# A linear-attention and gated-FFN kernel: another order of loading, casting and filling at the start, and a new order of the whole program

## The chip, the core and the metric

The kernel runs on one core of one Trainium2 chip. TensorE (PE) multiplies matrices into PSUM; its weight loads are listed as PEld. VectorE (DVE) and ScalarE (ACT) work element by element, GpSimd (POOL) hardly computes here and issues loads that also convert the type, and SyncE (SP) issues loads and stores. Each engine takes its instructions strictly in its own order and waits on semaphores for the others. The metric is the device time of one execution in microseconds (us).

## The reference

For 8 batches, 8 heads, 576 positions and a head size of 64, in float32:

```
kv  = einsum('bhsd,bhse->bhde', k, v)
out = einsum('bhsd,bhde->bhse', q, kv)
x   = out / sqrt(mean(out*out over e) + 1e-6) * g_norm        # heads side by side: 512 columns
h   = relu(x @ w_in)                                          # w_in 512 x 1024
c   = conv_w[0]*h[s-1] + conv_w[1]*h[s] + conv_w[2]*h[s+1]    # along positions, zero outside
y   = (h * sigmoid(c)) @ w_out                                # w_out 1024 x 512, float32 out
```

## The kernel before, in words

The program is written out as a list of some 850 short words, `ORDER` (lines 59 to 135). Each word calls a small function, for example `hk.0.1.0.0@4`: function `hk`, arguments batch 0, column block 1, half 0, part 0, and a place (a PSUM bank or a slot of a ring of buffers) behind the `@`. The last lines of the kernel tie each instruction to the one before it on its engine, so the order of the words is the order on every engine: no scheduler changes it.

One batch goes through these steps. `Lq`, `Lk`, `Lv` load q, k and v through POOL's queue, converting to bf16. `kv` multiplies k and v (64 x 64 products, L402), and `kva` (ACT, L416) or `kvd` (DVE, L414) copies the result to bf16. `qt` transposes q on PE (L433), `qd` or `qa` copies it. `ot` forms the output of attention (L460), `sq` squares it on ACT (L509), `on` or `oq` sums the squares with a matrix of ones on PE: `on` with two products on the whole array (L528), `oq` with four on quarters of it (L537). `nl` takes the reciprocal root on ACT (L545), `mo` multiplies on DVE and writes x (L556). A batch is cut into halves u (heads) and s (positions), so x has four quarters. `hk`, `hs` or `hm` multiply x by w_in (L658, L628, L613), and `rp`, `rh` or `re` apply relu on ACT. The convolution is `ta`, `aa`, `ab` on DVE (L681 to L692), for four blocks of batch 0 it is `cv` on PE (L708). `sg` (or `sc` after `cv`) is the sigmoid on ACT (L698, L715), `mg` the gate on DVE (L722), `om` the product by w_out, in two parts of four blocks (L732). `ea` or `ed` copies a row block out of PSUM on ACT or DVE (L738, L743), `st` stores it through SP's queue. `oh`, `eh`, `dh`, `sh` do the same in halves for the last row block. Batches 4 to 7 sum the squares of two batches at once (`ss`, `ln`, `sl`, `sp`, `mu`), and batches 6 and 7 transpose q by DMA (`tq`).

Batch 0 is special. Its q, k and v come in float32 through SP's and ACT's queues in the order of `HEAD` (line 233), in pieces: q in four (heads u, positions s; `q.1.0` is u = 1, s = 0), k in four, v in two. `cad` (DVE) and `caa` (ACT) convert them (L384, L386). POOL's loads, w_in first, start behind `gt.k.1.0`, a copy that waits for the piece k.1 (L378). Products of zeros that nobody reads, `fi` (L286), stand on PE between the steps of the start. `ct` transposes the convolution's weights, `pg` and `pc` prepare them, `dg` builds diagonal matrices for `cv`; `ps`, `pl` and `pn` build constants that are read much later, by batches 4 to 7.

Of the kernel before, what the change touches and what calls it, by code (L numbers as in the profile page):

```python
# [58 lines left out]
ORDER = """  # L59
pre@0,1 af cad.q.0.0@0 cad.v.0.0@0 fi.10.512@0 qt.0.0.0@2 qd.0.0.0@0 gt.k.1.0 Li.0.4 fi.9.512@0 ct@0 Lq.1.0.2@1  # L60
Lk.1.0.2@0 Lv.1.0.2@1 Li.4.4 ps pg fi.4.512@1 cad.k.1.0@1 caa.v.1.0 caa.k.0.0 kv.0.0.1@4 kva.0.0.1@0 ot.0.0.0@6 pc
cad.v.3.0 cad.k.2.0 fi.2.512@0 cad.k.3.0 caa.q.1.0 qt.0.1.0@2 qd.0.1.0@1 sq.0.0.0@0 oq.0.0.0@4 fi.2.512@0 dg.1
caa.v.2.0 kv.0.1.1@0 fi.2.512@2 nl.0.0.0@0 kva.0.1.1 ot.0.1.0@4 sq.0.1.0@1 cad.q.0.1 qt.0.0.1@2 qa.0.0.1 fi.2.512@0
oq.0.1.0@0 nl.0.1.0@1 mo.0.0.0@0 cad.q.1.1 qt.0.1.1@6 qd.0.1.1 mo.0.1.0 ot.0.0.1@2 sq.0.0.1@2 ot.0.1.1@6 fi.1.512@0
sq.0.1.1@3 oq.0.0.1@0 nl.0.0.1@2 fi.1.512@4 fi.1.512@4 hk.0.1.0.0@4 hk.0.1.0.1 rp.1.0@0 on.0.1.1@0 nl.0.1.1@3
hk.0.2.0.0@5 hk.0.2.0.1 rp.2.0 dg.3 mo.0.0.1 dg.2 hk.0.3.0.0@4 hk.0.3.0.1 hk.0.0.0.0@2 hk.0.0.0.1 rp.0.0 hk.0.0.1.0@3
rp.3.0 hk.0.1.1.0@5 hk.0.3.1.0@0 mo.0.1.1 hk.0.3.1.1 rp.3.1 hk.0.1.1.1 rp.1.1 hk.0.0.1.1 rp.0.1 dg.0 hk.0.2.1.0@1
hk.0.2.1.1 qt.1.0.0@6 kv.1.0.1@4 rp.2.1 cv.0.2@2 sc.0.2@0 cv.0.3@0 qd.1.0.0@2 kvd.1.0.1@1 ot.1.0.1@6 sc.0.3 pl
sq.1.0.1@4 cv.0.1@4 cv.0.0@2 Lq.1.2.2 Lk.1.2.2 Lv.1.2.2 sc.0.1@1 fi.2.512@0 qt.1.1.0@0 qd.1.1.0@3 mg.0.1.1 Lo.0.8
sc.0.0 mg.0.1.0 oq.1.0.1@4 nl.1.0.1@4 mo.1.0.1@1 fi.1.512@2 hk.0.5.1.0@2 hk.0.5.0.0@3 hk.0.5.0.1 rp.5.0 hk.0.5.1.1  # L70
rp.5.1 ta.0.1.5@0 hk.0.4.1.0@0 hk.0.4.1.1 rp.4.1 hk.0.7.0.0@1 hk.0.7.0.1 kv.1.1.1@4 kvd.1.1.1 rp.7.0 ot.1.0.0@2
sq.1.0.0@5 hk.0.7.1.0@6 hk.0.7.1.1 rp.7.1 ta.0.1.7@1 ot.1.1.1@0 sq.1.1.1@6 oq.1.0.0@4 nl.1.0.0@5 mo.1.0.0 hk.0.4.0.0@6
hk.0.4.0.1 rp.4.0 hk.0.6.1.0@7 hk.0.6.1.1 rp.6.1 oq.1.1.1@4 nl.1.1.1@6 mo.1.1.1 hk.0.6.0.0@6 Lq.2.0.4@2 hk.0.6.0.1
rp.6.0 ta.0.1.4 hk.1.6.1.0@7 ta.0.1.6 hk.1.0.1.0@2 ot.1.1.0@4 sq.1.1.0@7 aa.0.1.2 hk.1.1.1.0@3 hk.1.2.1.0@6 hk.1.6.1.1
rh.1.6.1 hk.1.1.1.1 rh.1.1.1 on.1.1.0@0 nl.1.1.0@7 mo.1.1.0 hk.1.2.1.1 hk.1.5.1.0@7 hk.1.5.1.1 rh.1.5.1 rh.1.2.1
hk.1.3.1.0@3 hk.1.3.1.1 rh.1.3.1 hk.1.0.1.1 rh.1.0.1 ab.0.1.2 sg.0.1.5 sg.0.1.4 qt.2.1.0@0 qt.2.0.0@6 hk.1.5.0.0@3
hk.1.5.0.1 rh.1.5.0 qd.2.0.0@4 hk.1.0.0.0@2 hk.1.4.1.0@4 hk.1.4.1.1 hk.1.0.0.1 hk.1.1.0.0@5 hk.1.6.0.0@6 hk.1.1.0.1
hk.1.2.0.0@7 hk.1.2.0.1 rh.1.2.0 rh.1.1.0 rh.1.0.0 hk.1.6.0.1 rh.1.6.0 aa.0.1.3 qd.2.1.0@0 ab.0.1.3 sg.0.1.7 sg.0.1.6
hk.1.7.0.0@0 mg.0.1.2 hk.1.7.1.0@1 hk.1.7.1.1 rh.1.7.1 hk.1.7.0.1 rh.1.7.0 ta.1.1.1@0 ta.1.1.0 Lk.2.0.4@1 Lv.2.0.4@0
Lq.3.0.4@0 Lk.3.0.4@0 Lv.3.0.4@1 Lq.4.0.4@1 aa.1.1.0 hk.1.4.0.0@3 om.0.1.0.4@2 rh.1.4.1 hk.1.4.0.1 rh.1.4.0  # L80
om.0.2.0.4@5 kv.2.0.2@6 mg.0.1.3 om.0.1.4.4 ab.1.1.0 sg.1.1.0 sg.1.1.1 kvd.2.0.2@2 ot.2.0.1@0 sq.2.0.1@0 ed.0.1@0
# [57 lines left out]
def kernel(  # L139
# [142 lines left out]
    @op  # L282
    def fi(n, w):
        ps = bank()
        for _ in range(n):
            nc.tensor.matmul(ps[:, :w], zero[:, :P], zero[:, :w], start=True, stop=True)  # L286
# [538 lines left out]
```

## Time and profile before

| | us |
|---|---|
| median of 3 runs (lowest to highest) | 177.75 (177.67 to 177.93) |
| span of the profiled execution, first to last instruction | 175.6 |
| difference, outside the span | 2.2 |
| PE, DVE, ACT busy | 167.9, 149.5, 148.9 |
| POOL busy | 22.2 |

The profile gives of the profiled execution its span, 175.6 us; what a timed run has beyond it lies ahead of the first and behind the last instruction, so changes are reckoned against the span and carried over to the median. A line of the timeline reads: start, duration, engine, line, operation, what it writes and reads, how many in a row, and in square brackets how long the engine stood idle and for whom. A line of the chain has start, duration, engine and line. A line of the stages has the stretch, its length, and for each engine the busy time and the number of instructions, then granted clock, busy share of the DMA engines and their GB/s.

### The profile page before, as it was taken

The numbers are of one execution on the slowest core, as the hardware profiler recorded it, in microseconds if no ns is written. First come the engines' busy times: TensorE is split into PE (matmuls) and PEld (weight loads), VectorE is DVE, ScalarE is ACT, GpSimd is POOL, SyncE is SP. The second block draws the span as 40 slices with busy tenths as digits, with TensorE's granted clock in tenths as the row PEclk, the third lists the DMA queues.
The fourth block names the chain that finished last, engine by engine and source line by source line (L and its number), as shares of the span: only waits on it lengthen the run. The fifth ranks groups of instructions, "written<-read, shape, count | busy, mean of one in ns | idle before, by whom it ended". The sixth has DMA issues, their size and how long they took to land.

```text
span 175.6 us, 5070 instructions
## 1 busy us (share of the span) xinstructions
PE 167.9 (96%) x2097; PEld 100.0 (57%) x2114; DVE 149.5 (85%) x290; ACT 148.9 (85%) x268; POOL 22.2 (13%) x35
## 2 busy tenths in 40 slices
PE   7979999999999999999999999999999999999992
PEld 2334766676447677644467764444877744444451
DVE  2796638899688899999999998989999999999950
ACT  2368899999978999999999998999999967676721
POOL 3094512200603013030000000000000000000000
PEclk9999999999999999999999999999999999999999
DMA  5999999999999999999999050330310003064486
GB/s 159 392 323 207 207 207 207 208 208 209 207 241 230 227 207 207 170 182 197 258 181 161 14 134 0 119 123 0 119 63 0 0 0 116 13 239 175 179 304 237
DMA packets 25911, 29.11 MB, mean 166 GB/s; under 512 B 6036, under 2 KB 20384, under 8 KB 25888
## 3 DMA queue, kind: packets, MB, share of 16 engines
q0 software_dynamic: 13296, 14.50, 49.2%
q1 hardware_dynamic: 12048, 13.11, 26.2%
q10 hardware_dynamic: 544, 1.18, 1.7%
q8 instruction: 16, 0.26, 0.6%
q14 instruction: 7, 0.06, 0.1%
HBM read 32.52 MB, written 9.44 MB: 239 GB/s over the span
## 4 chain that ended last, share of the span: by engine, by line
PE 76%; DVE 12%; ACT 5%; DMA 3%; issue 3%; ACTq 0%; DVEq 0%
PE banks L732 32%; PE banks L628 14%; PE banks L613 9%; PE banks L658 4%; DMA stg<-in_v_dram 3%; PE banks L460 3%; DVE h L722 2%; PE banks L708 2%; ACT taps L698 2%; PE banks L402 2%; PE banks L593 2%; PE banks L433 1%; PE banks L528 1%; DVE taps L681 1%; PE banks L286 1%
## 5 line engine op out<-in xcount | busy, mean ns | idle before, releaser
L732 PE MATMUL banks<-w_out_sb,h 128*128 128x512 bf16 x267 | 62.8, 379 | 1.2 <-issue 0.6
L698 ACT ACTIVATE taps<-taps,cw 128x576 bf16<-128x576 bf16 (+1 forms) x44 | 40.6, 958 | 5.7 <-DVE taps L692 5.5
L732 PEld LDWEIGHTS <-h 128*128 128x128 bf16 x280 | 26.2, 98 | 30.0 <-issue 1.1
L628 PE MATMUL banks<-x,w_in_sb 128*128 128x288 bf16 (+2 forms) x256 | 34.2, 286 | 0.0
L640 ACT ACTIVATE h<-banks 128x288 bf16<-128x288 f32 (+2 forms) x80 | 29.5, 460 | 0.3 <-PE banks L658 0.2
L628 PEld LDWEIGHTS <-w_in_sb 128*128 128x128 bf16 x256 | 24.4, 98 | 7.8 <-issue 0.8
L722 DVE TENSOR_TENSOR h<-h,taps 128x1152 bf16<-128x1152 bf16 (+1 forms) x24 | 22.8, 952 | 1.2 <-ACT taps L698 1.2
L687 DVE TENSOR_TENSOR taps<-taps 128x1152 bf16<-128x1152 bf16 (+1 forms) x22 | 21.5, 978 | 0.5
L509 ACT ACTIVATE sq<-banks 128x576 bf16<-128x576 f32 (+2 forms) x32 | 20.8, 691 | 1.1 <-PE banks L460 1.1
L692 DVE TENSOR_TENSOR taps<-taps,h 128x1152 bf16<-128x1152 bf16 (+1 forms) x22 | 21.4, 972 | 0.3
L681 DVE TENSOR_SCALAR taps<-h,cw 128x576 bf16<-128x576 bf16 (+1 forms) x44 | 18.7, 424 | 0.6 <-ACT h L665 0.5
L682 DVE TENSOR_SCALAR taps<-h,cw 128x576 bf16<-128x576 bf16 (+1 forms) x44 | 18.4, 418 | 0.0
L738 ACT ACTIVATE row<-banks 128x512 f32<-128x512 f32 x23 | 13.5, 597 | 5.7 <-PE banks L732 4.2
L658 PE MATMUL banks<-x,w_in_sb 128*128 128x288 bf16 (+2 forms) x128 | 17.7, 286 | 0.1
L613 PE MATMUL banks<-x,w_in_sb 128*128 128x288 bf16 x128 | 16.9, 286 | 0.0
L556 DVE SCALAR_TENSOR_TENSOR x<-banks,cw,rs 128x576 bf16<-128x576 f32 (+2 forms) x16 | 13.0, 816 | 3.9 <-ACT rs L545 3.6
L658 PEld LDWEIGHTS <-w_in_sb 128*128 128x128 bf16 x128 | 12.0, 98 | 4.4 <-issue 0.5
L227 ACT ACT_TABLE_LOAD x10 | 12.8, 1283 | 2.0 <-issue 1.8
L613 PEld LDWEIGHTS <-w_in_sb 128*128 128x128 bf16 x128 | 12.3, 98 | 3.7 <-issue 0.2
L443 DVE COPY qT<-banks 128x1152 bf16<-128x1152 bf16 (+2 forms) x13 | 8.8, 681 | 5.7 <-PE banks L433 5.7
L545 ACT ACTIVATE rs<-banks,eps_sb 128x576 f32<-128x576 f32 (+2 forms) x16 | 11.8, 740 | 1.1 <-PE banks L528 1.1
L599 DVE SCALAR_TENSOR_TENSOR x<-o,cw,banks 128x576 bf16<-128x576 f32 (+2 forms) x16 | 12.1, 810 | 0.7 <-PE banks L593 0.5
(89 smaller groups left out, 162.9 us busy)
## 6 DMA issues: line engine op xcount, KB each, us to landing
out_dram<-row SPq DMA_DIRECT2D x35, 256.0 KB, 2.3
q_sb<-in_q_dram POOLq DMA_DIRECT2D x6, 576.0 KB, 17.9
k_sb<-in_k_dram POOLq DMA_DIRECT2D x6, 576.0 KB, 14.5
v_sb<-in_v_dram POOLq DMA_DIRECT2D x6, 576.0 KB, 17.9
stg<-in_v_dram ACTq DMA_DIRECT2D x2, 576.0 KB, 6.2
stg<-in_k_dram SPq DMA_DIRECT2D x4, 288.0 KB, 6.9
w_in_sb<-in_moe_w_in_dram POOLq DMA_DIRECT2D x2, 512.0 KB, 9.9
w_out_sb<-in_moe_w_out_dram POOLq DMA_DIRECT2D x1, 1024.0 KB, 15.5
```

Of the source, the lines that this page charges most:

```text
L509: nc.scalar.activation(T["sq", b, u, s], T["o", b, u, s], AX.Square)
L613: nc.tensor.matmul(ps[:, s, :HS], w_in_sb[:, t, f * P:(f + 1) * P], T["x", b][:, t, c0:c1], start=(t == 0), stop=(t == NT - 1))
L628: nc.tensor.matmul(ps, w_in_sb[:, t, f * P:(f + 1) * P], T["x", b][:, t, c0:c1], start=(t == 0), stop=(t == NT - 1))
L640: nc.scalar.activation(h, fr, AX.Relu)
L658: nc.tensor.matmul(T[at], w_in_sb[:, t, f * P:(f + 1) * P], T["x", b][:, t, c0:c1], start=(t == 0), stop=(t == NT - 1))
L681: nc.vector.tensor_scalar_mul(tap[:, 0, f % 2, :n, 8:8 + S], h[:, f], cw[:, f:f + 1])
L682: nc.vector.tensor_scalar_mul(tap[:, 1, f % 2, :n, :S], h[:, f], cw[:, 2 * NF + f:2 * NF + f + 1])
L687: nc.vector.tensor_add(tap[:, 1, :, :n, :S], tap[:, 0, :, :n, 7:7 + S], tap[:, 1, :, :n, 1:1 + S])
L692: nc.vector.tensor_add(y, y, span(b, n)[:, 2 * j:2 * j + 2])
L698: nc.scalar.activation(y, y, AX.Sigmoid, scale=cw[:, NF + f:NF + f + 1])
L722: nc.vector.tensor_mul(h, h, tap_of(b, j)[:, 1, :, :n, :S])
L732: nc.tensor.matmul(T["om", p, m], h[:, f, m * P:(m + 1) * P], w_out_sb[:, f, :], start=(f == 0), stop=(f == NF - 1))
```

## The change

The words of `ORDER` are put in another order from the first to the last, and some are exchanged for others. The parts that can be named:

- SP's queue at the start loads k.2 and k.3 ahead of q.1.0 (`HEAD`).
- The first half of w_in is loaded by two instructions of two column blocks each (`Li.0.2`, `Li.2.2`) where there was one of four. Behind it POOL loads v, k, q of batch 1 (it was q, k, v), and later the whole of batch 2's q, v, k ahead of w_out (it was w_out first).
- Seven converting copies of the start are on ACT and five on DVE (it was four and eight); `qa.0.0.0` copies the first transposed q on ACT. `pl`, `pn` and `ps` stand at DVE's start.
- A new word, `ff`, is like `fi` with float32 operands. The products of zeros are now `ff.4.256`, `ff.3.256`, `ff.1.128`, `ff.2.256`, `ff.1.128`, `ff.1.192`, `ff.1.256` and, on bf16, seven `fi` words, all ahead of the first `hk`. Before, `fi` words of 34 products of 512 columns stood ahead of it and three behind.
- Six `on` words became `oq`; `kva` and not `kvd` copies for batches 2, 3 and 6; `ea` took the place of `ed` for five row blocks, `ed` of `ea` for four.
- `oq` and `on` take one bank where the result fits in one (`pair`). The functions `ad` and `y_of` are new, but no word calls `ad`, so they change nothing that runs.

```diff
 ORDER = """
-pre@0,1 af cad.q.0.0@0 cad.v.0.0@0 fi.10.512@0 qt.0.0.0@2 qd.0.0.0@0 gt.k.1.0 Li.0.4 fi.9.512@0 ct@0 Lq.1.0.2@1
...
+pre@0,1 af pl pn ps caa.q.0.0@0 caa.v.0.0@0 ff.4.256@0 qt.0.0.0@0 qa.0.0.0@0 caa.k.0.0@0 cad.v.1.0 ff.3.256@2
+ff.1.128@2 ct@0 pg pc caa.k.1.0 gt.k.1.0 Li.0.2 caa.v.2.0 ff.2.256@1 ff.1.128@1 kv.0.0.1@2 Li.2.2 dg.1 kva.0.0.1@0
...
+    def pair(n):
+        if 2 * n <= 512:
+            return bank()[:, :2 * n].rearrange("p (e n) -> p e n", e=2)
+        return bank2()[:, :, :n]
...
-    HEAD = (("sync", "q.0.0 k.0.1 k.1.1 q.1.0 k.2.1 k.3.1 q.0.1 q.1.1"), ("scalar", "v.0.2 v.2.2"))
+    HEAD = (("sync", "q.0.0 k.0.1 k.1.1 k.2.1 k.3.1 q.1.0 q.0.1 q.1.1"), ("scalar", "v.0.2 v.2.2"))
...
     @op
+    def ff(n, w):
+        ps, z = bank(), zero.bitcast(FP32)
+        for _ in range(n):
+            nc.tensor.matmul(ps[:, :w], z[:, :P], z[:, :w], start=True, stop=True)
...
     def on(b, u, s):
         c0, c1 = cols(b, s)
-        ps = T["on", b, u, s] = bank2()[:, :, :c1 - c0]
+        ps = T["on", b, u, s] = pair(c1 - c0)
...
     def oq(b, u, s):
         c0, c1 = cols(b, s)
-        ps = T["on", b, u, s] = bank2()[:, :, :c1 - c0]
+        ps = T["on", b, u, s] = pair(c1 - c0)
```

Where the instructions stand now is shown at three places.

ACT at the start, before: the loads of v, the table of functions, then the copies of batch 0 (`v_sb`, `k_sb` and `q_sb` are the bf16 copies of the float32 pieces `stg` and `stq`, `kvb` the copied product of k and v, `sq` the squares, `rs` the reciprocal root).

```order
L227 ACT_TABLE_LOAD
L386 ACTIVATE v_sb<-stg 128x576
L386 ACTIVATE k_sb<-stg 128x576
L416 ACTIVATE kvb<-banks 128x2x64
L386 ACTIVATE q_sb<-stq 128x2x256
L509 ACTIVATE sq<-banks 128x2x256
L386 ACTIVATE v_sb<-stg 128x576
L545 ACTIVATE rs<-banks,eps_sb 128x2x256
```

The same place now:

```order
L232 ACT_TABLE_LOAD
L398 ACTIVATE q_sb<-stq 128x2x256
L398 ACTIVATE v_sb<-stg 128x576
L457 ACTIVATE qT<-banks 128x2x256
L398 ACTIVATE k_sb<-stg 128x576 x2
L398 ACTIVATE v_sb<-stg 128x576
L428 ACTIVATE kvb<-banks 128x2x64
L398 ACTIVATE k_sb<-stg 128x576
L521 ACTIVATE sq<-banks 128x2x256
```

The first q, two more pieces of k and the copy of the transposed q (`qT`) moved in ahead of the first squares; a piece of q moved behind.

DVE at the start, before, from the float32 identity on (`bg` and `spread` are the constants of `ps`, `cw` the convolution's weights):

```order
L280 CAST ident_65<-ident 25x25
L384 CAST q_sb<-stq 128x2x256
L384 CAST v_sb<-stg 128x576
L443 COPY qT<-banks 128x2x256
L326 TENSOR_TENSOR bg<-ident 128x8
L330 TENSOR_TENSOR bg<-bg,ident 128x8 x10
L331 COPY spread<-bg 128x512
L295 COPY cw<-banks 128x25
L384 CAST k_sb<-stg 128x576
```

The same place now (`sel` is of `pl`; `ng`, `nb`, `na` are of `pn`):

```order
L286 CAST ident_65<-ident 25x25
L329 MEMSET sel 128x64
L333 MEMSET sel 64x3 x8
L348 TENSOR_REDUCE ng_81<-ident 128x1
L348 TENSOR_REDUCE ng_82<-ident 128x1
L349 TENSOR_SCALAR nb<-ng_82 128x1
L350 TENSOR_SCALAR na<-ng_81 128x1
L351 TENSOR_TENSOR na<-na,nb 128x1
L338 TENSOR_TENSOR bg<-ident 128x8
L342 TENSOR_TENSOR bg<-bg,ident 128x8 x10
L343 COPY spread<-bg 128x512
L396 CAST v_sb<-stg 128x576
```

The constants moved ahead of every copy of the inputs, and three of those copies left this stretch.

POOL's loads, before, from the second half of w_in on:

```order
L361 DMA w_in_sb<-in_moe_w_in_dram 128x4x512
L347 DMA q_sb<-in_q_dram 128x2x576
L347 DMA k_sb<-in_k_dram 128x2x576
L347 DMA v_sb<-in_v_dram 128x2x576
L365 DMA w_out_sb<-in_moe_w_out_dram 128x8x512
L347 DMA q_sb<-in_q_dram 128x4x576
L347 DMA k_sb<-in_k_dram 128x4x576
L347 DMA v_sb<-in_v_dram 128x4x576
```

The same place now:

```order
L373 DMA w_in_sb<-in_moe_w_in_dram 128x4x512
L359 DMA q_sb<-in_q_dram 128x2x576
L359 DMA k_sb<-in_k_dram 128x2x576
L359 DMA v_sb<-in_v_dram 128x2x576
L359 DMA q_sb<-in_q_dram 128x4x576
L359 DMA v_sb<-in_v_dram 128x4x576
L359 DMA k_sb<-in_k_dram 128x4x576
L377 DMA w_out_sb<-in_moe_w_out_dram 128x8x512
```

w_out moved behind the three loads of batch 2.

More of the change, by code (lines that the diff above doesn't have):

```diff
@@ L65 @@
[L65 to L74, printed above, removed]
@@ L408, in kvc @@
     def kvc(eng, b, u0, n):
-        if u0 == 0:
+        if ("kvb", b) not in T:
             T["kvb", b] = ring("kvb", [P, 2, 2 * D], BF16, "kvb")
```

158 lines of the change are left out of this document (90 added, 68 removed).

## The prediction

> **What bounds the kernel now.** I read the busy shares first, then the stages, then the timeline of the start, then the chain's end. The page's busy times, and the six stages that I cut (start to first `hk`, to the first product by w_out, to batch 4's k·v product, to the last x, to the last gate, to the end):
>
> ```profile
> span 175.6 us, 5070 instructions
> PE 167.9 (96%) x2097; PEld 100.0 (57%) x2114; DVE 149.5 (85%) x290; ACT 148.9 (85%) x268; POOL 22.2 (13%) x35
> ...
> 0.00:16.86 16.86, 14.30 (x204) 6.00 (x208) 11.18 (x48) 8.65 (x15) 7.91 (x16) 1.00 0.97 273
> 16.86:41.10 24.24, 24.00 (x396) 17.25 (x397) 17.45 (x42) 23.05 (x47) 6.11 (x8) 1.00 1.22 207
> 41.10:66.86 25.76, 25.35 (x491) 16.17 (x491) 21.88 (x43) 23.89 (x47) 5.20 (x7) 1.00 1.20 221
> 66.86:121.50 54.64, 53.74 (x708) 31.10 (x715) 52.08 (x77) 54.03 (x92) 2.96 (x4) 1.00 0.78 136
> 121.50:166.60 45.10, 44.94 (x271) 26.36 (x273) 44.26 (x80) 37.28 (x68) 0.00 (x0) 1.00 0.24 88
> 166.60:172.60 6.00, 5.59 (x34) 3.13 (x32) 2.64 (x5) 1.91 (x4) 0.00 (x0) 1.00 0.84 310
> ```
>
> From 16.86 us on PE never stands for long: its idle time over the five later stages is 0.24 + 0.41 + 0.90 + 0.16 + 0.41 = 2.1 us. But the other engines are nearly as full: ACT is idle 0.6 us in the fourth stage, DVE 0.8 us in the fifth, and the DMA engines are saturated (share 1.2) until 66.86. So the time is the start up to the first `hk`, plus PE's work, and there is little room for any engine to do more. The start is the one stage that is not full of useful work:
>
> ```profile
> 1.20 4.45 PE L286 MATMUL banks<-zero 128*128 128x512 bf16 x10 [1.20 <-DVE zero L265]
> 4.98 0.43 DVE L384 CAST q_sb<-stq 128x512 bf16<-128x512 f32 x1 [1.92 <-DMA stq<-in_q_dram]
> 5.57 0.32 PE L433 MATMUL banks<-ident,q_sb 64*64 64x64 bf16 x16
> 5.83 2.12 PE L286 MATMUL banks<-zero 128*128 128x512 bf16 x9
> 6.86 0.68 ACT L386 ACTIVATE k_sb<-stg 128x576 bf16<-128x576 f32 x1 [0.55 <-DMA stg<-in_k_dram]
> 7.87 0.24 PE L291 MATMUL banks<-ident,cw_rows 25*128 25x25 f32 x1
> 8.04 1.04 PE L286 MATMUL banks<-zero 128*128 128x512 bf16 x4
> 8.35 0.19 POOL L378 COPY gate<-stg 128x1 f32<-128x1 f32 x1 [5.49 <-DMA stg<-in_k_dram]
> 8.93 0.59 DVE L384 CAST k_sb<-stg 128x576 bf16<-128x576 f32 x1
> 10.10 0.28 ACT L416 ACTIVATE kvb<-banks 128x128 bf16<-128x128 f32 x1 [2.55 <-PE banks L402]
> 12.30 0.48 PE L402 MATMUL banks<-v_sb,k_sb 64*64 64x64 bf16 x36
> 14.70 0.69 ACT L545 ACTIVATE rs<-banks,eps_sb 128x512 f32<-128x512 f32 x1
> 16.42 0.39 PE L286 MATMUL banks<-zero 128*128 128x512 bf16 x1
> 16.86 0.60 PE L658 MATMUL banks<-x,w_in_sb 128*128 128x256 bf16 x4
> ```
>
> To be seen here: the piece k.1 has landed by 8.35 (POOL's gate), but DVE, still busy with `ps`, converts it at 8.93 to 9.52; the second k·v product follows only at 12.30; and products of zeros stand on PE to the end.
>
> **The start, part by part.** *Casts on ACT.* k.1 lands as before. ACT is free for it: 8.35 + 0.68 = 9.03, against 9.52, so the first k·v product begins 0.4 us earlier. On DVE the constants now fill the wait that ends at 4.98, so they are hidden by the first load; without that cover they would cost what they cost before, the 0.58 us between 8.35 and 8.93. *k.2 and k.3 ahead of q.1.0.* They land between 8.35 and 11.0; ACT converts k.2 behind `kva` (about 10.0 to 10.7), DVE k.3 by 11.0. The second k·v product then stands at 11.1 and not 12.30, 1.2 us earlier. q.1.0 comes later by two pieces, still ahead of its transpose at about 12. *What is late next* is ACT, in order: copy of k·v, root, a cast of q.0.1 (0.75 us), squares, copy of q, root. Adding these up from 11.1, the root that stands at 14.70 begins at about 14.4. Of 1.2 us 0.3 is left, and two products of zeros go (16.42 and its neighbour): the first `hk` at 16.2 and not 16.86. *w_in in two loads.* The first `hk` needs only the first quarter, which lands earlier than the half did, so it does not hold this back.
>
> *The float32 products.* No float32 product of this width is in the trace. The bounds of one with 256 columns, warm: 0.12 us, half of the 2.12/9 = 0.236 us of a bf16 one of 512; and 1.74 us, from the 25-column float32 product that holds PE from 7.87 to 8.04, 0.17 us or 6.8 ns a column. I take the geometric middle, 0.46 us. Then 3.5 of them (with the 128-column one) end at 6.0 + 1.6 = 7.6, before the transpose at 7.87, and 2.5 more at 8.1 + 1.15 = 9.25, 0.15 us beyond the cast of k.1: they hide in the waits. Break-even is 0.53 us each for the first group. The Trainium skill, page "FP8 and Floating Point Precision", section "TensorE Precision Notes", gives float32 four passes through the array; an estimate by it is 4 × 0.118 = 0.47 us, and the sum would be the same.
>
> **After the first `hk`.** Rows for this part, from the timeline, the list of DMA issues (us to landing at the end), the chain and the groups (busy us, mean ns):
>
> ```profile
> 17.87 0.78 ACT L545 ACTIVATE rs<-banks,eps_sb 128x640 f32<-128x640 f32 x1
> 25.31 0.38 PE L286 MATMUL banks<-zero 128*128 128x512 bf16 x1
> 26.48 0.39 PE L286 MATMUL banks<-zero 128*128 128x512 bf16 x1
> 27.60 0.74 ACT L545 ACTIVATE rs<-banks,eps_sb 128x576 f32<-128x576 f32 x1
> 16.87 0.91 POOL L365 DMA_DIRECT2D w_out_sb<-in_moe_w_out_dram  x1 [2.30 <-DMA w_in_sb<-in_moe_w_in_dram]
> w_out_sb<-in_moe_w_out_dram POOLq DMA_DIRECT2D x1, 1024.0 KB, 15.5
> 41.10 1.03 PE L732 MATMUL banks<-w_out_sb,h 128*128 128x512 bf16 x3
> 31.78 0.43 PE banks L537 x4
> 49.40 0.24 PE banks L528 x2
> L414 DVE CAST kvb<-banks 128x256 bf16<-128x256 f32 (+1 forms) x8 | 3.1, 387 | 0.4 <-PE banks L479 0.2
> L321 DVE MEMSET sel<- 64x3 bf16 x8 | 0.5, 61 | 0.4
> L336 DVE TENSOR_REDUCE ng<-ident 128x1 f32<-128x32 bf16 x2 | 0.3, 178 | 0.0
> L313 DVE TENSOR_SCALAR diag<-ident,cw 128x128 bf16<-128x128 bf16 x8 | 1.9, 303 | 0.0
> L743 DVE COPY row<-banks 128x512 f32<-128x512 f32 x12 | 8.2, 687 | 1.6 <-PE banks L732 1.6
> 165.91 0.75 DVE L722 TENSOR_TENSOR h<-h,taps 128x1152 bf16<-128x1152 bf16 x1
> 162.94 7.50 PE banks L732 x34
> 170.44 1.76 PE banks L757 x16
> ```
>
> *Three fills gone.* 0.7 us of PE, but ACT's root at 27.60 gates what follows. ACT's work up to it is the same, and its root at 17.87 comes only 0.1 us earlier, so I put it at 27.35. By 28.7 us the lead is 0.7 us, the start's, and no more.
>
> *`oq` for `on`.* Five of the six stand behind that point; 0.43 against 0.24 us where it stands alone, nothing where it joins other quarter-array products: 0 to 0.95 us, I take 0.3.
>
> *w_out behind batch 2.* It landed at 16.87 + 15.5 = 32.4. Three loads of 576 KB (0.59 MB) at the stage's 207 GB/s take 8.5 us: 40.9 now. The first `om` stood at 41.10; 0.9 us of work (a k·v product and two products by w_in) moved ahead of it, and with the lead it is due at 41.1 + 0.9 − 0.7 = 41.3. That is 0.4 us behind the landing; smaller pieces of w_in may load slower, and PE may win back idle time ahead of it. A wait of 0 to 0.9 us; I take 0.2. Batch 4's v, seven loads on, lands at 60.9, and its k·v product, moved up past 4.6 us of other work, is due at 66.86 − 4.6 − 0.7 = 61.6: covered by 0.7 us.
>
> *DVE.* Behind x's last quarter of batch 0 DVE loses `pl`, `pn`, a pair of diagonals and three copies of k·v, and gets two row copies more (0.69 each): three copies at 0.39 and 0.5 + 0.3 + 2 × 0.3 of constants less 1.4, 1.2 us net. At the end it gives back: behind the last gate (165.91 to 166.66) PE has 16 products of 7.50/34 = 0.22 us and 1.76 us of halves; now 20 and the same, 0.9 us more. Net −0.3 us on the engine that ends the fifth stage, before any of its own 3.4 us of idle time in the last two long stages is won back; I take 0.3 of that. ACT takes the copies: with `ea` for one `ed` about +1.4 us up to the second `ln`.
>
> *PE's idle time* of 2.1 us: a new order may win back 0 to 1.3 us, or add as much; I take −0.5.
>
> Sum on PE's line: −0.7 + 0.3 + 0.2 − 0.5 = −0.7 us; on DVE's, with the 0.1 us of the root at 17.87: −0.1 − 0.3 − 0.3 = −0.7. The span of 175.6 becomes 174.9, and with the same 2.2 us outside it the median 177.75 becomes 177.0, 0.4% less.
>
> **The rivals.** *A, the order fits fully* (18%): no wait for w_out, PE's idle time won back, the lead of 1.3 us that PE has at 25 us kept. −1.3 − 1.3 + 0.6 = −2.0: about 175.8 to 176.5. For it: all four lines get shorter at the start. Against it: ACT has 0.6 us of idle time in 54.64.
>
> *B, the loads eat it* (12%): the two quarter loads of w_in cost 0.5 us, each later load shifts, PE waits 0.9 us at the first `om`. 177.7, no change.
>
> *C, PE stays cold* (18%, slower). The first row of the start has ten products in 4.45 us, its fourth nine in 2.12: PE's rate doubled about 4.4 us after it began, with no gap. Now the first fill is four float32 products, at the cold rate 4 × 0.92 = 3.7 us, so PE stands from 4.9 to about 5.7. If that gap costs the faster rate until about 9 us, the next fills take twice their time, the first k·v product begins at 10.6 and not 9.1, 1.0 us after the old place, and the first `hk` near 17.9: 177.75 + 1.0 = 178.7. It decides from 0.5 us per warm product on. The Trainium skill, page "TensorE: Matmul & The Clock Gate", section "What's actually happening", says that the full clock comes after a window of about 3.4 us of sustained activity, and that the window does not start with the kernel. The trace's 4.4 us agrees; by that rule a gap of 0.8 us inside the window may delay it by one window, which is this rival.
>
> *D, ACT ends last* (18%, slower). ACT has 1.4 us more to do up to the second `ln` and 0.6 us idle in 66.86:121.50. If PE and DVE then wait for its relus: 1.4 − 0.6 less 0.1 from the earlier root, +0.7: 178.4. Against it: behind 121.5 ACT has 7.8 us to spare, and the earlier stages have 1.2 and 1.9.
>
> **How the numbers follow.** What stands in the sum 34% (176.6 to 177.4), A 18, B 12, C 18, D 18. A change below 0.2% (0.36 us), about what this measurement can tell, is B alone. Faster: 34 + 18 = 52; same 12; slower 36. The range runs from 175.9 (most of A) to 178.8 (C with D's excess left out), which leaves out about 2 in 10.
>
> **What the changed profile would show.** The first `hk` at 16.2; the first k·v copy on ACT at about 9.7, the second k·v product at 11.1; `om` beginning at 40.9 behind a wait for w_out or none; the last gate near 165.3; no engine with a longer wait than before in 66.86 to 121.5. A first k·v product after 9.6 would make C right, a PE that waits for ACT in the fourth stage D, and a row of L298 longer than 0.53 us, warm, would overturn the price of the fills.

## The result

The changed kernel takes 184.86 us in the median of four runs (184.39 to 185.84), the kernel before 177.84 beside it; the ratio is 1.040 (95% interval 1.036 to 1.043), 7.0 us slower. The profiled execution took 185.84 us with a span of 183.4, so it lies 1.0 us above the median, and what follows reads it for places, not for the last half microsecond.

Span and busy times of the changed kernel's page, and its stages (start to first `hk`, to batch 4's k·v product, to the wait at 91.6, the wait, the stretch behind it, to the last gate, to the end; columns as in the table of the prediction):

```profile
span 183.4 us, 5111 instructions
PE 173.1 (94%) x2123; PEld 104.3 (57%) x2123; DVE 147.1 (80%) x283; ACT 153.8 (84%) x275; POOL 22.8 (12%) x36
```

```profile
0.00:18.10 18.10, 15.84 (x208) 10.60 (x208) 11.78 (x62) 10.78 (x18) 9.67 (x19) 1.00 1.02 266
18.10:64.75 46.65, 45.98 (x794) 29.02 (x792) 34.35 (x59) 43.88 (x88) 9.45 (x13) 1.00 1.21 217
64.75:91.63 26.88, 25.74 (x501) 15.53 (x501) 23.37 (x38) 26.22 (x51) 3.72 (x5) 1.00 1.29 164
91.63:94.72 3.09, 0.00 (x1) 0.03 (x1) 0.81 (x1) 0.22 (x1) 0.00 (x0) 1.00 1.26 177
94.72:99.40 4.68, 4.67 (x29) 2.44 (x29) 3.68 (x5) 4.12 (x5) 0.00 (x0) 0.64 1.76 282
99.40:173.58 74.18, 74.14 (x559) 43.05 (x557) 71.96 (x117) 66.36 (x111) 0.00 (x0) 1.00 0.25 86
173.58:183.40 9.82, 6.71 (x39) 3.61 (x37) 1.11 (x2) 2.18 (x4) 0.00 (x0) 1.00 0.42 156
```

PE's busy time grew by 5.2 us, although it does nearly the same work: part of it ran at the half clock (0.64 in the fifth row; the first row's 1.00 only means that no change was recorded yet). Three places are to be seen. The start is 1.24 us longer. In the third stage PE is idle 1.14 us. In the fourth it stands for 3.09 us, and behind that the clock is down.

*The start*, in the timeline of the changed kernel:

```profile
1.19 3.78 PE L298 MATMUL banks<-zero 128*128 128x256 f32 x8 [1.19 <-DVE zero L271]
5.82 0.43 PE L445 MATMUL banks<-ident,q_sb 64*64 64x64 bf16 x16 [0.85 <-ACT q_sb L398]
6.18 3.35 PE L298 MATMUL banks<-zero 128*128 128x256 f32 x8
11.46 0.48 PE L414 MATMUL banks<-v_sb,k_sb 64*64 64x64 bf16 x36
13.25 0.48 PE L414 MATMUL banks<-v_sb,k_sb 64*64 64x64 bf16 x36
18.10 1.05 PE L670 MATMUL banks<-x,w_in_sb 128*128 128x256 bf16 x8
5.14 0.63 ACT L398 ACTIVATE q_sb<-stq 128x512 bf16<-128x512 f32 x1 [2.04 <-DMA stq<-in_q_dram]
```

Each float32 product is recorded as two. Four of them take 3.78 us cold and end at 4.97; ACT ends q's cast at 5.77 (DVE ended it at 5.41 before), and PE stands 0.85 us. The second group of eight records takes 3.35 us: it is still cold. The trace's record of the clock turns to full at 10.71 us; in the kernel before it did at 5.62. That is rival C, with the first k·v product at 11.46 (C: 10.6) and the first `hk` at 18.10 (C: 17.9).

*The middle.* Pieces of the chain, the wait in PE's timeline, and SP's issues, of the changed kernel:

```profile
67.07 1.03 issue
...
76.74 17.95 DMA qT<-q_sb
```

```profile
94.72 0.33 PE L512 MATMUL banks<-qT,kvb 64*64 64x320 bf16 x4 [3.09 <-DMA qT<-q_sb]
```

```profile
69.77 11.36 SPq L479 DMA_TRANSPOSE qT<-q_sb  x2
81.47 9.59 SPq L773 DMA_DIRECT2D out_dram<-row  x5
91.16 1.95 SPq L501 DMA_DIRECT2D kvx<-kvb  x2
```

The same queue in the kernel before:

```profile
65.92 2.16 SPq L467 DMA_TRANSPOSE qT<-q_sb  x1
79.87 5.41 SPq L748 DMA_DIRECT2D out_dram<-row  x3
85.64 1.18 SPq L489 DMA_DIRECT2D kvx<-kvb  x2
86.91 5.98 SPq L467 DMA_TRANSPOSE qT<-q_sb  x2
```

The new order has both transpositions of batch 6's q (`tq.6.1`, then `tq.6.0`) together, ahead of the row stores, in the stretch in which the loads of batches 5 to 7 fill the DMA engines. Before, the second stood behind the stores and ran when the loads had nearly ended. The second now takes 17.95 us from issue to landing, and it is the one that PE needs first. What that does to the loads is seen in the data rate (last column, GB/s), first of the kernel before, then of the changed one:

```profile
76.00:82.00 6.00, 1.00 1.27 183
82.00:88.00 6.00, 1.00 1.17 245
```

```profile
76.00:82.00 6.00, 1.00 1.36 134
82.00:88.00 6.00, 1.00 1.34 129
```

The engines are as busy as before and move 134 where it was 183, and 129 where it was 245 (no transposition is under way there in the kernel before). The last load lands at 102.1 us and not at 92.9.

Two things are in that. The first is taking turns. In the trace's list of packets a transposition is 1152 packets of 256 bytes, a load 512 packets of 1152 bytes. In the kernel before, between 72 and 78 us, 807 of the first and 785 of the second kind passed, one for one, at 32 and 106 ns each, and the loads moved 151 GB/s where they move 205 alone (changed kernel, 66 to 72 us). The Trainium skill, page "DMA: Bandwidth & Descriptors", section "Queues, rings and completion order", says that each engine goes round the queues that have work, a packet at a time; these counts agree with that. Whether such a packet is one entry of the trace's list is not shown. In the changed kernel the counts are less even, 409 and 245 between 76 and 78 us, 266 and 255 between 90 and 92. The second is that the packets themselves take longer in the changed kernel: between 82 and 88 us a packet of a load took 141 ns and one of a transposition 78 ns, and the loads moved 99 GB/s. Why they take longer is not shown.

### The profile page after: what moved, and what is told of

The parts are those of the page before. It is cut to its first block, busy times and chain, and to the rows that moved or that the text cites. A ratio compares the mean times of both kernels' runs of the same rounds, so it can differ in the third digit from the quotient of the medians.

```text
span 183.4 us, 5111 instructions
## 1 busy us (share of the span) xinstructions
PE 173.1 (94%) x2123; PEld 104.3 (57%) x2123; DVE 147.1 (80%) x283; ACT 153.8 (84%) x275; POOL 22.8 (12%) x36
## 4 chain that ended last, share of the span: by engine, by line
PE 79%; DMA 12%; ACT 5%; issue 2%; ACTq 0%
PE banks L757 29%; PE banks L640 17%; DMA qT<-q_sb 10%; PE banks L625 9%; PE banks L670 8%; PE banks L298 3%; DMA stq<-in_q_dram 2%; PE banks L414 2%; PE banks L472 2%; PE banks L445 2%; PE banks L549 2%; ACT taps L738 1%; ACT sq L521 1%; PE banks L605 1%; PE banks L782 1%
## 5 line engine op out<-in xcount | busy, mean ns | idle before, releaser
L757 PE MATMUL banks<-w_out_sb,h 128*128 128x512 bf16 x280 | 64.0, 379 | 0.0
L640 PE MATMUL banks<-x,w_in_sb 128*128 128x288 bf16 (+2 forms) x256 | 34.4, 286 | 1.1 <-issue 1.0
L763 ACT ACTIVATE row<-banks 128x512 f32<-128x512 f32 x24 | 14.4, 599 | 7.6 <-PE banks L757 5.3
L521 ACT ACTIVATE sq<-banks 128x576 bf16<-128x576 f32 (+2 forms) x32 | 20.0, 666 | 0.4 <-PE banks L472 0.4
L693 DVE TENSOR_SCALAR taps<-h,cw 128x576 bf16<-128x576 bf16 (+1 forms) x44 | 18.7, 426 | 0.4 <-ACT h L652 0.3
L694 DVE TENSOR_SCALAR taps<-h,cw 128x576 bf16<-128x576 bf16 (+1 forms) x44 | 18.7, 424 | 0.0
L670 PE MATMUL banks<-x,w_in_sb 128*128 128x288 bf16 (+2 forms) x128 | 18.6, 287 | 0.0
L625 PE MATMUL banks<-x,w_in_sb 128*128 128x288 bf16 x128 | 18.0, 300 | 0.0
L533 ACT ACTIVATE o<-banks 128x576 f32<-128x576 f32 (+2 forms) x16 | 10.1, 660 | 3.4 <-PE banks L512 3.3
```

Of the source, the lines that this page charges most:

```text
L521: nc.scalar.activation(T["sq", b, u, s], T["o", b, u, s], AX.Square)
L625: nc.tensor.matmul(ps[:, s, :HS], w_in_sb[:, t, f * P:(f + 1) * P], T["x", b][:, t, c0:c1], start=(t == 0), stop=(t == NT - 1))
L640: nc.tensor.matmul(ps, w_in_sb[:, t, f * P:(f + 1) * P], T["x", b][:, t, c0:c1], start=(t == 0), stop=(t == NT - 1))
L670: nc.tensor.matmul(T[at], w_in_sb[:, t, f * P:(f + 1) * P], T["x", b][:, t, c0:c1], start=(t == 0), stop=(t == NT - 1))
L693: nc.vector.tensor_scalar_mul(tap[:, 0, f % 2, :n, 8:8 + S], h[:, f], cw[:, f:f + 1])
L694: nc.vector.tensor_scalar_mul(tap[:, 1, f % 2, :n, :S], h[:, f], cw[:, 2 * NF + f:2 * NF + f + 1])
```

## The experiments

Times are medians; the kernel before stood at 177.7 beside each. Two pairs of causes were in question: for the start the gap or the type of the products, for the middle the transpositions, the loads, or ACT.

**Which transposition first.**

```diff
-tq.6.1@4 ... tq.6.0@0
+tq.6.0@4 ... tq.6.1@0
```

> The changed kernel with one thing different: SP issues the transposition of batch 6's first half of heads (tq.6.0) first and that of its second half (tq.6.1) second; they also exchange their buffers, so nothing else moves. Theory 'the second of two': in the changed kernel tq.6.0 was issued at 76.74 us, as the second, and landed 17.95 us later; PE waited 3.1 us for it and then ran at half clock from 96.0 to 99.4 (1.7 us lost). With the order exchanged tq.6.0 is issued at about 69.8 and lands near 83, before its product is due at 91.6; tq.6.1 lands near 94.7 and is due only about 8 us behind. No wait, no half clock: 184.9 - 4.8 = 180.1 us. Rival 'the DMA engines are simply late': the traffic as a whole is behind by then, so the wait moves to the next reader (tq.6.1's product or batch 7's) and the time stays within 1 us of 184.9.

183.74 us (181.26 to 185.13). In the profiled execution, the slowest of the four, the wait went from its place and came back at the next reader:

```profile
101.46 0.43 PE L512 MATMUL banks<-qT,kvx 64*64 64x256 bf16 x4 [3.40 <-DMA kvx<-kvb]
```

The regrouped copy of k·v (`kvx`, issued at 90.1) stands in SP's queue behind the second transposition, which landed at 92.7, and behind five row stores whose packets passed only from 91 us on; it landed at 101.4. In this execution the rival is right: the order of the two is not the cause. The fastest of the four, 181.26, is as fast as the run that follows here, and has no profile, so how much the exchange alone is worth, 1.1 us in the medians, stays open.

**One transposition out of the stretch of loads.**

```diff
-tq.6.1@4 ... tq.6.0@0 ... kx.6@0
+tq.6.0@4 ... kx.6@0 tq.6.1@0
```

> The changed kernel with batch 6's first transposition (tq.6.0) issued first, at about 69.8 us, and its second one (tq.6.1) taken out of the stretch of loads: SP issues it behind the row stores and behind the regrouped k·v copy of batch 6 (kx.6), at about 85 to 91 us, where the kernel before had it. PE's and POOL's rows stay as they are. Theory 'packets one for one': while a transposition and a load are both under way, the DMA engines take a packet of 256 bytes of the one and a packet of 1152 bytes of the other in turn (76 to 78 us in the changed kernel: 245 load packets, 409 of transpositions), so two transpositions of 1152 packets each hold up the loads by about their own duration: the last load lands at 102.1 and not at 92.9. With one of them out of the stretch the last load lands near 95, both products of batch 6 find their data, no wait over 0.5 us between 85 and 105 and no half clock there: about 3.1 + 1.7 us less, 180 us, and 178.5 where the start has its full clock early. Rival 'the loads are too many for the new order': the last load still lands at about 100 and PE waits as long for another tile; 183 to 185.

181.48 us (180.40 to 181.77): 3.4 us less than the changed kernel, by the exchange of the run before and one DMA instruction moved; 2.3 of it are beyond the exchange alone. PE no longer waits there, the clock stays full from 10.6 us on, and the loads run again (window 82 to 88):

```profile
91.53 0.33 PE L512 MATMUL banks<-qT,kvb 64*64 64x320 bf16 x4
```

```profile
82.00:88.00 6.00, 1.00 1.21 224
```

The last load lands at 94.7. It is less than the 4.8 us that were expected; between the two profiled executions it is 4.2 (spans of 183.4 and 179.2), and what takes the rest is not shown. With one transposition left in the loads the long packets are still there for a while: between 78 and 82 us a packet of a load took 216 ns.

**The same fault put into the kernel before.**

```diff
-tq.6.0@1 st.0.8 ... kx.6@0 tq.6.1@3
+tq.6.0@1 tq.6.1@3 st.0.8 ... kx.6@0
```

> The kernel before with one thing of the change alone: SP issues batch 6's second transposition (tq.6.1) directly behind its first one, ahead of the row stores, so at about 76 to 80 us inside the stretch of loads, and not at 87 to 93. PE, DVE, ACT and POOL keep their rows. Theory 'packets one for one': the loads fall behind from there, the last lands at 97 to 102 us and not at 92.9, PE waits for it or for batch 7's transpositions at about 97 to 108, 2 to 5 us: 180 to 183 us. Rival 'the transposition's place does no harm, the load order did': batch 6's transpositions are both early, nothing waits: 177.7 within 0.4.

179.19 us (177.89 to 179.74), ratio 1.007 (1.004 to 1.010). PE stands for batch 6's v:

```profile
86.24 0.77 PE L479 MATMUL banks<-v_sb,k_sb 64*64 64x64 bf16 x72 [1.78 <-DMA v_sb<-in_v_dram]
```

That a transposition moved in among the loads makes them late is shown here by itself: batch 6's v landed at 86.1 us and not at 83.6, the last load at 95.6 and not at 92.9. The price is under the 2 to 5 us that were expected: 1.5 in the medians, nothing in two of the ten times (177.9). Two things differ from the changed order: nothing reads the second transposition before 96 us, and the packets keep their length for most of the stretch (31 and 106 ns between 80 and 84 us), so that the engines move 176 GB/s between 82 and 88 and not 129. The halved rate is not reproduced by the place alone.

**The fill.** Its gap closed with the type of before, and with float32:

```diff
-ff.4.256@0
+fi.10.512@0        # one run
+ff.5.256@0         # another
```

> The changed kernel with its first fill exchanged for that of the kernel before: ten bf16 products of 512 columns in place of four float32 products of 256. Nothing else. Theory 'cold through the gap': the full clock comes near 5.6 us again and not at 10.7, the first product by w_in stands at about 16.2 to 16.9 and not 18.1: 1.2 to 1.9 us less, 183.0 to 183.7 us. Rival 'the start is late for another reason' (the order of the casts on ACT, the float32 products behind the first): the clock comes early, but the first product by w_in stays later than 17.5 and the time changes by less than 0.6 us.

> The changed kernel with five float32 products in the first fill where it had four; one takes 2 x 0.43 us here while PE is cold, so the fill ends near 5.83 where q's cast ends at 5.77: the gap of 0.85 us is closed with products of the same type. If the gap is what delayed the clock, it is full at about 5.6 us and the time is that of the bf16 fill within 0.3 us (183.0 to 183.7). If it is the type (float32 products not counted as activity, or only in part), the clock stays half until about 10 us and the time stays at 184.9 within 0.5.

183.91 us (183.50 to 184.27) and 184.63 (184.23 to 184.84). In the second, without a gap, the same eight records behind the transpose are warm:

```profile
6.12 1.78 PE L298 MATMUL banks<-zero 128*128 128x256 f32 x8
```

So float32 products count as activity. But ten bf16 products ended at 5.08 in their profiled run, which had turned warm at 4.4, a gap of 0.70 was left, and it did no harm; and of two kernels with the unchanged fill the one of the exchanged transpositions came out warm, the one with the late transposition cold:

```profile
5.75 0.32 PE L445 MATMUL banks<-ident,q_sb 64*64 64x64 bf16 x16 [0.78 <-ACT q_sb L398]
6.00 1.78 PE L298 MATMUL banks<-zero 128*128 128x256 f32 x8
```

```profile
5.66 0.43 PE L445 MATMUL banks<-ident,q_sb 64*64 64x64 bf16 x16 [0.69 <-ACT q_sb L398]
6.02 3.35 PE L298 MATMUL banks<-zero 128*128 128x256 f32 x8
```

With a gap the early clock is a matter of chance, run by run. Of the twenty profiles of this document the fifteen whose first fill is long enough to last, at the cold rate, to 5.6 us or beyond have the full clock by 7.0 us; of the five with a shorter one three have it only behind 10.1. Neither run gained much in time, 0.95 and 0.2 us: PE came earlier to 62 us and stood there for loads, 1.34 and 1.47 us.

**A gap in the kernel before, short and long.**

```diff
-fi.10.512@0
+fi.8.512@0         # one run
+fi.4.512@0         # another
```

> The kernel before with eight bf16 products in its first fill where it had ten, so that PE stands from about 4.8 us to the first transpose at about 5.3 to 5.6, a gap of 0.5 to 0.9 us, with no float32 product of this size anywhere. If the gap is what delays the clock, the full clock moves from 5.6 to about 10 us and the first product by w_in from 16.86 to about 18: 178.7 to 179.1 us. If the type does it, the kernel is as before, 177.8 within 0.3.

> The kernel before with four bf16 products in its first fill where it had ten: PE works from 1.2 to 3.0 us and then stands until the first transpose at about 5.5, so that it comes into the start at half clock in every run, and not by chance as with eight products (177.7 in two of ten runs, 179.0 to 179.2 in three, 182 to 185 in five). Theory 'the cold start costs its own 1.3 us': clock full only at 9 to 10.8 us, the first product by w_in near 18.2, the rest as before: 178.9 to 179.3 us. Rival 'a late PE is punished again later' (a transposition that it now meets inside the loads, a wait of some us and a spell at half clock): 182 to 185 us, with a gap on PE behind 60 us.

With eight products the ten times lie between 177.70 and 184.98 (median 180.66); the profiled one, at 177.77, was warm at 4.1 us in spite of a gap of 1.06. With four, PE is cold in the profiled run, and all four times lie between 182.47 and 184.96 (median 184.53, ratio 1.034, 1.028 to 1.041): 6.8 us, of which the start itself is 1.64 (all later issues on POOL stand that much later). The rest is a wait for batch 6's v at 86 us, and two spells of half clock behind it (the profile names ACT, long done by then; v, issued at 70.3, landed at 89.0):

```profile
89.12 1.18 PE L479 MATMUL banks<-v_sb,k_sb 64*64 64x64 bf16 x72 [3.15 <-ACT taps L698]
```

```profile
88.70:95.50 6.80, 6.05 (x95) 0.50 0.93 152
```

The rival "a late PE is punished again later" is right. v was issued 1.64 us later than in the kernel before and landed 5.4 us later: between 72 and 78 us, with the first transposition under way in both, the engines moved 109 GB/s and not 188. The transposition begins when q has landed, which PE does not move (65.89 and 65.92 us), so the loads that PE releases stand otherwise to it; that this is why the packets take longer is argued, not shown. Why three of the ten times with eight products stand at 179.0 to 179.2, only the start's part above, is not settled.

**Late transposition and closed fill together.**

```diff
-ff.4.256@0
+fi.11.512@0
```

> The kernel of the run before with the first fill of eleven bf16 products of 512 columns (cold 11 x 0.445 = 4.9 us, from 1.2 to 6.1), so that PE has no gap ahead of the first transpose at 5.8. Theory 'both causes': the clock is full between 4.0 and 6.1 in every run, the first product by w_in at about 16.3; then PE comes to batch 4's k·v product (k and v landed at 64.0) about 1.3 us too early, as with the bf16 fill alone, and gains only what is left: 178.5 to 179.5 us and a smaller spread than without the fill. Rival as for the run before: 183 to 184.

181.10 us (180.37 to 181.92), 1.6 above the range that was expected. The first `hk` stands at 15.99, 0.87 us ahead of the kernel before, but PE then stands for loads:

```profile
64.09 0.77 PE L414 MATMUL banks<-v_sb,k_sb 64*64 64x64 bf16 x72 [1.37 <-DMA v_sb<-in_v_dram]
...
77.61 0.77 PE L414 MATMUL banks<-v_sb,k_sb 64*64 64x64 bf16 x72 [1.08 <-DMA v_sb<-in_v_dram]
```

Of the 2 us that warm and cold start differ at the first `hk` 0.4 are left in the medians, which is within the spread of either run.

**The loads in another order**, on top of that: v of batch 5 ahead of v of batch 6; then q of batch 5 behind k and v of batch 4; then batch 5's transposition on PE away from the 72 products of batch 4's k·v.

```diff
-Lv.6.0.4@1 ... Lv.5.0.4@0
+Lv.5.0.4@1 ... Lv.6.0.4@0
...
-Lq.5.0.4@1 ... Lv.4.0.4@0
+Lv.4.0.4@0 Lq.5.0.4@1
...
-qt.5.0.0@2 hs.2.3.0@7 ... hs.3.2.0@4 qd.5.0.0@1 ... hs.2.6.0@5
+hs.2.3.0@7 ... hs.3.2.0@4 qt.5.0.0@2 ... hs.2.6.0@5 ... qd.5.0.0@1
```

> The kernel with the late transposition and the closed fill (181.1 us), and besides batch 5's v loaded in the place of batch 6's v and the other way round (the two exchange their buffers too). In the changed kernel v of batch 5 takes the buffer that batch 4's k·v product frees, so it is issued only at 65.9 us, behind v of batch 6 that nobody reads before 89, and PE stood 1.08 us for it at 76.5 in the run with the closed fill. Theory 'loads in the wrong order': that wait goes, 180.0 to 180.3 us. Rival 'ACT is the bound from 88 us on' (in that run's chain ACT has most of the pieces from 88 to 110): PE is earlier at 77 but not at 110, and the time stays at 181.1 within 0.4.

> As the run before, and besides batch 5's q loaded behind batch 4's k and v, not ahead of them. PE stood 1.37 us at 62.7 for batch 4's k and v, which landed at 64.0; a load of 576 KB takes 2.8 us of the saturated queue (208 GB/s), so they land at 61.2 now and the wait goes; q of batch 5 lands at 64.0, ahead of its transposition on PE at about 64.5. Theory 'loads in the wrong order': another 1.0 to 1.4 us, 178.8 to 179.3 us in all, unless PE now stands about 1 us at 65 to 66 for its own instructions, as in the changed kernel at 67.07. Rival 'ACT is the bound from 88 us on': 180.5 to 181.3.

> As the run before, and besides batch 5's first transposition of q on PE (36 products, qt.5.0.0) four products by w_in behind the place where it stood, 9 and 14 words behind batch 4's k·v product (72 products) for it and its copy. In the changed kernel PE stood 1.03 us at 67.07, 'issue' in the chain, waiting for nothing that the profile shows, 1.2 us behind 108 small products and as many weight loads in a row; the queue that loads instructions brought 16 KB at 65.66 and landed at 66.64. Theory 'PE ran out of instructions': with the small products spread that stall shrinks to under 0.4 us, up to 0.8 us less time than the run before where it had the stall. Rival: the stall belongs to something else (a buffer of PSUM) and stays, or wanders with the words; no change within 0.3 us.

183.57, 184.38 and 183.69 us: all worse. The exchange had a fault: v of batch 7 now needs the buffer of batch 6's v, which is read only at 88 us. Its load moved from 78.7 to 88.5, beside the transpositions, and PE waited for one of those:

```profile
88.54 0.74 POOL L359 DMA_DIRECT2D v_sb<-in_v_dram  x1 [16.12 <-PE banks L491]
```

```profile
100.45 0.30 PE L512 MATMUL banks<-qT,kvx 64*64 64x256 bf16 x4 [2.95 <-DMA qT<-q_sb]
```

It is the third time that a load beside a transposition costs about 3 us of wait (3.09 in the changed kernel, 3.15 in the cold run above). With batch 7's v in the other buffer:

```diff
-Lv.7.0.4@0
+Lv.7.0.4@1
```

> The run with batch 5's v first, and besides batch 7's v in the buffer that batch 5 leaves (free at about 78 us) and not in batch 6's, which held it back to 88.5 us. Theory 'loads in the wrong order': the loads end near 92, the wait of 1.08 us at 76.5 is gone and none of 3 us at 97.5 follows: 180.0 to 180.3 us. Rival 'PE's and ACT's order from 88 us on is the bound': 181.1 within 0.4, with ACT in the chain from 88 to 110.

> As the run before, with batch 5's q behind batch 4's k and v. Theory 'loads in the wrong order': the wait at 62.7 goes too, except 0.6 us at the transposition of batch 5's q and 0.4 us of 'issue' that the earlier run of this order showed: 179.3 to 179.8 us. Rival: 181.1 within 0.4.

> As the run before, with the transposition of batch 5's q four products by w_in later on PE. In the earlier pair of runs PE's gaps of 0.63 and 0.37 us around 64 to 66 became one of 0.72 us, so 0 to 0.3 us less than the run before: 179.0 to 179.8. Rival: 181.1 within 0.4.

179.86 us (179.79 to 180.29), 180.18 (179.83 to 180.46) and 179.59 (179.43 to 180.18; ratio 1.011, 1.008 to 1.014). The order of the v loads is worth 1.2 us, as expected; q's order nothing (179.3 to 179.8 was expected); the spread of small products between 0 and 0.6. The stall of 1.03 us at 67.07 comes in sizes of 0.2 to 0.7 us around 65 us in these runs and no profile shows what it waits for; "PE ran out of instructions" is not shown.

**What is left above the kernel before**, 1.9 us. Behind the last gate the best of these takes 9.85 us (167.35 to 177.2), the kernel before 8.94 (166.66 to 175.6): 0.9. From 90 to 109 us its chain runs over ACT, a part of it (the kernel before has PE's products there):

```profile
90.51 0.70 ACT sq L521
91.21 0.70 ACT taps L721
91.91 0.33 issue
92.24 0.65 ACT h L631
...
105.56 2.29 ACT taps L721 x2
107.85 1.09 ACT h L631 x2
```

```diff
-kva.2.0.2@0 ... kva.3.0.2@0 ... kva.6.0.2@0
+kvd.2.0.2@0 ... kvd.3.0.2@0 ... kvd.6.0.2@0
```

> The best of the changed orders (179.6 us) with the copies of the k·v product of batches 2, 3 and 6 on DVE, as the kernel before had them, and not on ACT. Theory 'ACT ends last from 90 to 109 us': ACT has 0.4 us less to do at batch 6 and 0.8 us less ahead of it, so 0.3 to 0.5 us less, 179.1 to 179.3 us. Rival 'DVE is as full there' (21.4 of 21.5 us busy, ACT 21.2): DVE's chain takes the place of ACT's, 179.6 within 0.2, or up to 0.4 us more.

180.29 us (179.68 to 180.49), 0.7 more in the medians, though the two spreads overlap. The theory's gain did not come. ACT's lead in the chain does not mean that DVE has room: the window 90.47 to 112.00 of that run has DVE at 21.36 and ACT at 21.31 of 21.53 us, which fits the rival; where the last 1.0 us lies in the order stays open.

**The start alone, ahead of the kernel before.** Loads of k first; then the whole start up to the first `hk`; then up to batch 0's relus.

```diff
-    HEAD = (("sync", "q.0.0 k.0.1 k.1.1 q.1.0 k.2.1 k.3.1 q.0.1 q.1.1"), ("scalar", "v.0.2 v.2.2"))
+    HEAD = (("sync", "q.0.0 k.0.1 k.1.1 k.2.1 k.3.1 q.1.0 q.0.1 q.1.1"), ("scalar", "v.0.2 v.2.2"))
```

> The kernel before with one thing of the change alone: SP loads k.2 and k.3 of batch 0 ahead of q.1.0. Its casts keep their places, so k.2 and k.3 are there earlier for DVE, and q.1.0's cast on ACT (behind the copy of the first k·v product, at about 10.4) finds its piece only at about 11. The prediction's step 'second k·v product at 11.1 and not 12.30, first product by w_in earlier by a part of it' without the other parts. If that step holds: second k·v product at 11.5 to 12.0, first product by w_in at 16.5 to 16.9, 177.4 to 177.8 us. If the order of the casts on ACT and DVE sets the start and not the landing: ACT waits 0.5 us for q.1.0, the first product by w_in stays at 16.86 or comes at 17.3, 177.7 to 178.3 us; and if a late PE is punished again as in the cold start, up to 180.

178.53 us (178.34 to 181.67, two of five above 181): 0.7 us slower by itself. ACT, whose casts kept their order, now stands for q.1.0, and the first `hk` is at 17.48. The full clock came at 7.0 us in that profile and not at 5.6, but the copy of the first k·v product is only 0.07 us late (10.17 for 10.10), so nearly all of the 0.6 us at the first `hk` is ACT's wait and what follows from it:

```profile
10.88 0.63 ACT L386 ACTIVATE q_sb<-stq 128x512 bf16<-128x512 f32 x1 [0.43 <-DMA stq<-in_q_dram]
```

> The kernel before from the first product by w_in on, with the start of the change ahead of it: k.2 and k.3 ahead of q.1.0, the seven casts on ACT, constants first, w_in's first half in two loads, float32 fills, with the first fill as eleven bf16 products so that there is no gap. The loads of batch 1 stay in their old order, w_out ahead of batch 2. With this start and the changed order behind it the first product by w_in stood at 15.99 (16.86 in the kernel before). Theory 'the start was right once PE is warm': first product by w_in at 16.0, and with only the start ahead of DMA-paced work the kernel gains 0.3 to 0.9 us: 176.8 to 177.4 us. Rival 'the lead is given back': ACT's root or the loads hold PE by 28 us or by 66, 177.7 within 0.3. Rival 'an early PE meets the transpositions otherwise', as a late one does: over 178.3.

178.46 us (178.30 to 184.50), with three of ten times above 183. Where the two orders join, PE stands 0.58 us at 15.3 for DVE's copy of the transposed q, and the first `hk` came at 17.22 in the profiled execution (178.41). The three long ones have no profile; that a late PE was punished again in them is not shown.

> As the run with the start alone, but the change's order (with the closed first fill) reaches to the last relu of batch 0's first four column blocks, so that the banks of the start are those of the changed kernel; from the first transposition of batch 1 on stands the kernel before, with its loads of batch 1 and 2 and of w_out. Theory 'the start was right once PE is warm': first product by w_in at 16.0 to 16.6 and not 16.86 or 17.22, 177.0 to 177.5 us. Rival 'the lead is given back at ACT's root near 28 us or at the loads': 177.7 within 0.3. Rival 'PE and the transpositions fall out of step': over 178.3, or runs of 182 to 185 between the others.

177.84 us (177.74 to 178.39 in ten), ratio 1.0011 (0.9999 to 1.0022): no change. The first `hk` stands at 16.03, 0.83 us ahead, and ACT's root, which gates the stretch that follows, at 27.35, where the kernel before has it at 27.60:

```profile
16.03 1.05 PE L670 MATMUL banks<-x,w_in_sb 128*128 128x256 bf16 x8
...
27.35 0.74 ACT L557 ACTIVATE rs<-banks,eps_sb 128x576 f32<-128x576 f32 x1
```

From there nearly every later issue on POOL and SP is 0.2 to 0.4 us early. In the profiled execution ACT's last copy still begins 0.26 us earlier (172.01 for 172.27), but the last store takes 3.5 us behind that copy where it took 2.9, so at the end nothing is left. No version that was run beats the kernel before.

## Why the prediction was wrong

Forecast: 177.0, range 175.9 to 178.8. Measured: 184.9, outside it and on the other side.

*The step that failed: the sum had no term for what was moved on SP's queue.* The four transpositions and their place among the loads do not occur in it; the loads were priced by landing and due time in POOL's queue alone, and "no engine with a longer wait than before in 66.86 to 121.5" became a wait of 3.09 us. Exchanging two of them and moving one back gives 3.4 of the 7.0 us (the exchange alone 1.1, not clear of its spread), and moving one forward in the kernel before costs 1.5. Why the packets of transposition and loads take so much longer in the changed order stays open.

*"w_out behind batch 2 … batch 4's v lands at 60.9, due at 61.6, covered by 0.7."* w_out landed at 41.3 (forecast 40.9) and nobody waited for it. Batch 4's v landed at 64.0, 3.1 us late: the seven loads were counted at the stage's rate, with the row stores between 50 and 60 us, which share the engines, left out (four were issued from 47.6 us on; between 50 and 61 us the loads landed 3.6 to 4.2 us apart, and 2.8 on either side). With a warm start PE stood 1.37 us for it. That batch 5's v had been put behind batch 6's, for lack of a buffer, was not priced at all; it is worth 1.2 us.

*The start, "first k·v product at 9.1, second at 11.1, first `hk` at 16.2".* Right where PE is warm: 9.33, 11.12 and 15.99. *Float32 products at 0.46 us, warm:* four took 1.78 us, 0.445 each. (The second group was to end 0.15 us behind the cast of k.1; by the prediction's own 9.25 and 9.03 it is 0.22.) What the sum left out is the gap that its own rival C names, 4.9 to 5.7 (measured 4.97 to 5.82): four cold products were in C and not in the likeliest case. C was right in mechanism, at 18%, and in places nearly: the first `hk` at 18.10 for 17.9, the first k·v product at 11.46 for 10.6. Whether it happens in an execution is chance, and it has no fixed size in the total, 0.4 us in one order and 6.8 in another.

*"The lead is 0.7 by 28.7."* The root was put at 27.35 behind one that was to come 0.1 us earlier, which would give 27.5. With a warm start it stood at 27.52 in the changed order, and at 27.35 with the changed start alone; so 27.35 was met only there. Either way the lead is what the root gained, 0.1 to 0.25, and not the start's 0.7. The prediction wrote both sentences.

*"Tail 0.9 us longer behind the last gate."* 9.82 against 8.94: right. *"DVE net −0.3"* came to nothing, because DVE did not end the fifth stage: the last gate began at 172.82 behind PE's waits.

*"PE's idle time −0.5."* It became 4.95 us behind the first `hk`, against 1.69 by the same count: 3.09 for the transposition, 1.03 at 67.07.

*Rival D, ACT ends last.* In the changed kernel it is hidden by the waits; with them removed, ACT does carry most of the chain for 19 us. But DVE is as full, and D's sum (copies moved to ACT) is not borne out: moved back, they gained nothing and cost 0.7 in the medians.

By undoing, in the order in which it was done: the transpositions 3.4, the gap in the fill 0.4, the v loads 1.2, q and the small products 0.3. Of these only 3.4 and 1.2 are clear of the spread. What is left, 1.9, is not undone by any run: 0.9 of it is the tail as read from two profiles, and 1.0 no run accounts for. In another order the shares would be others, since each wait hides the next.

## What to carry to other kernels

Price a moved DMA as two things, its own landing and what it does to every transfer that is in flight beside it. A transposition beside loads cost them here a quarter of their rate where its small packets only took turns with theirs, and half where the packets grew longer too, so it belongs where the loads have ended or far ahead of its reader. Make the first fill long enough to reach, at the cold rate, the end of the first cast, since a shorter one leaves the early clock to chance. A lead at the start is worth what is left of it at the next gate of another engine, here 0.25 of 0.83 us.
